# Second w1 block issued from ScalarE's queue, and six h groups instead of four on the first 256 rows

## The chip, the cores and the metric

The kernel runs on one core of one Trainium2 chip. The metric is the device time of one execution in microseconds, as the median of several executions. All ratios compare a kernel with executions of the kernel before on the same chip in the same rounds.

## The reference

A dense layer with Silu, forward and backward, in bf16, with x of 2048 × 640, w1 of 640 × 1536 and w2 of 1536 × 640:

```python
h = jnp.einsum("bsd,df->bsf", x, w1)
a = jax.nn.silu(h)
out = jnp.einsum("bsf,fd->bsd", a, w2)
# and the gradients of out for x, w1 and w2, given grad_out
```

## The kernel before

The chip's engines are named: TensorE multiplies matrices, ScalarE and VectorE work element by element, SyncE issues loads. "The engines" without a name are the 16 DMA engines, which move the data; a load "lands" when the last of them has reported its part, and an engine that is far behind the others is called a straggler. A "queue" or "ring" is the list of loads that one issuing engine has handed to them.

The kernel goes through the 2048 rows in four chunks of 512. For each chunk it computes h (12 groups of 128 columns of w1, each with 5 matmuls over D = 5 × 128), then Silu and its derivative, then the output and the gradient of x. The two weight gradients follow. Only the start matters here: the first chunk has to wait for its loads. All of them go through SyncE's queue, in this order:

```python
early += load_x() + [load_w1_rows(0, 1), load_w1_rows(1, 3)]   # x rows 0-255; w1 rows, columns 0-511
load_w1_rows(3, DT)
nc.sync.dma_start_transpose(out=xT_next[:, :, HC:SC], in_=x2[HC:SC, :])   # x rows 256-511, transposed
start_before_entry_wait(nc, {i.ins.name for i in early})
for fc in range(1, NFC):
    load_w1(fc * FC, (fc + 1) * FC)                            # second and third block of 512 columns
nc.scalar.activation(warm_a[:], warm[:, 0:1], ACT.Silu)        # brings the table in early
nc.sync.dma_start(out=w2_nat[:], in_=w2_v[:])
```

TensorE begins with what arrives first: h groups 0 to 3 on the first 256 rows ("half-width" matmuls, 256 columns wide), then the same groups on the other 256 rows, then groups 4 to 11 at full width (512):

```python
def h_first(xT, aT, ghT):
    # ... one tile each for the first FB = 4 groups ...
    for dt_ in range(DT):
        for ft in range(FB):
            h_mm(hps[ft], ft, xT, dt_, dt_ + 1, slice(0, HC))
    for i in range(FT + LAG_G):
        if i < FT:
            if i < FB:
                h_mm(hps[i], i, xT, 0, DT, slice(HC, SC))
            else:
                # ... a new tile ...
                h_mm(hps[i], i, xT, 0, DT)
            silu_a(i, hps[i], aT)
        # ... the derivative of group i - LAG_G ...
```

"Rows 1 and 2" and "rows 3 and 4" below are the second and third of the three loads of w1 rows (row blocks 1-2 and 3-4 of five). "The block" is the second column block of w1, which groups 4 to 7 need.

Of the kernel before, what the change touches and what calls it, by code (L numbers as in the profile page):

```python
# [9 lines left out]
ACT = mybir.ActivationFunctionType  # L10
# [5 lines left out]
def start_before_entry_wait(nc, names):  # L16




    def move(nc):
        blocks = nc.m.functions[0].blocks
        entry, home = blocks[0].instructions, blocks[1].instructions
        for engine in {i.engine for i in home if i.name in names}:
            mine = [i for i in home if i.engine == engine]
            last = max(k for k, i in enumerate(mine) if i.name in names)
            moved = mine[: last + 1]
            gate = next(
                k
                for k, i in enumerate(entry)  # L30
                if i.engine == engine and isinstance(i, mybir.InstEventSemaphore)
            )
            taken = {i.name for i in moved}
            for k in reversed(range(len(home))):
                if home[k].name in taken:
                    del home[k]
            for i in reversed(moved):
                entry.insert(gate, i)

    nc.at_finalize(move)  # L40

# [21 lines left out]
def kernel(  # L63
# [11 lines left out]
    nc = tc.nc  # L75
# [9 lines left out]
    ST, DT, FT = S // P, D // P, F // P  # L85
# [3 lines left out]
    FC = 512  # L89
    NFC = F // FC  # L90
    FB = FC // P
    LAG = 2
    LAG_G = 4
    NWARM = 24
    HC = 2 * P
    dt_in = x.dtype

# [14 lines left out]
    w1_v = w1.rearrange("(dt p) f -> p dt f", p=P)  # L112
# [19 lines left out]
    with ExitStack() as mctx:  # L132
# [7 lines left out]
        warm = cpool.tile([P, P], dt_in, name="warm")  # L140
        early = [nc.vector.memset(warm[:], 1.0)]
        warm_a = cpool.tile([P, 1], FP32, name="warm_a")
        wp = ps_h.tile([P, SC], FP32, name="wp", tag="hp")
        for i in range(NWARM):
            early.append(nc.tensor.matmul(wp[:, 0:P], lhsT=warm[:], rhs=warm[:], start=True, stop=True))
# [4 lines left out]
        w1_nat = w1pool.tile([P, DT, F], dt_in, name="w1_nat", tag="w1a")  # L150
# [14 lines left out]
        xT_next = xpool.tile([P, DT, SC], dt_in, name="xT")  # L165
        x_two = cpool.tile([P, 2, D], dt_in, name="x_two")

        def load_w1(lo, hi):
            nc.sync.dma_start(out=w1_nat[:, :, lo:hi], in_=w1_v[:, :, lo:hi])

        def load_x():
            return [nc.sync.dma_start(out=x_two[:], in_=x2[0:HC, :].rearrange("(p q) d -> p q d", q=2))]

        def load_w1_rows(lo, hi):
            return nc.sync.dma_start(out=w1_nat[:, lo:hi, 0:FC], in_=w1_v[:, lo:hi, 0:FC])  # L175

        early += load_x() + [load_w1_rows(0, 1), load_w1_rows(1, 3)]
        load_w1_rows(3, DT)
        nc.sync.dma_start_transpose(out=xT_next[:, :, HC:SC], in_=x2[HC:SC, :])  # L179
        start_before_entry_wait(nc, {i.ins.name for i in early})  # L180
        for fc in range(1, NFC):
            load_w1(fc * FC, (fc + 1) * FC)
        nc.scalar.activation(warm_a[:], warm[:, 0:1], ACT.Silu)
        nc.sync.dma_start(out=w2_nat[:], in_=w2_v[:])
        goT_next = load_goT(0)
        for fc in range(NFC):
# [3 lines left out]
        for dt_ in range(DT):  # L190
# [3 lines left out]
            copy_tp = nc.scalar.copy if dt_ % 2 else nc.vector.tensor_copy  # L194
            copy_tp(out=xT_next[:, dt_, 0:HC], in_=tp[:].rearrange("p q s -> p s q"))

        def h_mm(hp, ft, xT, lo, hi, cols=slice(0, SC)):
            for dt_ in range(lo, hi):
                nc.tensor.matmul(  # L199
                    hp[:, cols],  # L200
                    lhsT=w1_nat[:, dt_, ft * P:(ft + 1) * P],
                    rhs=xT[:, dt_, cols],
                    start=(dt_ == 0),
                    stop=(dt_ == DT - 1),
                )

        def silu_a(ft, hp, aT):
            nc.scalar.activation(aT[:, ft, :], hp[:], ACT.Silu)  # L208

        def silu_grad(ft, hp, aT, ghT):  # L210
            t = tpool.tile([P, SC], FP32, name="t")
            nc.scalar.activation(t[:], hp[:], ACT.Tanh, scale=0.5)  # L212
            v = tpool.tile([P, SC], dt_in, name="v")
            nc.vector.tensor_scalar(out=v[:], in0=t[:], scalar1=-0.5, scalar2=0.5, op0=ALU.mult, op1=ALU.add)  # L214
            nc.vector.scalar_tensor_tensor(  # L215
                out=ghT[:, ft, :], in0=aT[:, ft, :], scalar=1.0, in1=v[:], op0=ALU.subtract, op1=ALU.mult
            )
# [6 lines left out]

        def h_first(xT, aT, ghT):
            hps = []
            for ft in range(FB):
                hps.append(ps_h.tile([P, SC], FP32, name="hp"))
            for dt_ in range(DT):
                for ft in range(FB):  # L230
                    h_mm(hps[ft], ft, xT, dt_, dt_ + 1, slice(0, HC))
            for i in range(FT + LAG_G):
                if i < FT:
                    if i < FB:
                        h_mm(hps[i], i, xT, 0, DT, slice(HC, SC))
                    else:
                        hps.append(ps_h.tile([P, SC], FP32, name="hp"))
                        h_mm(hps[i], i, xT, 0, DT)
                    silu_a(i, hps[i], aT)
                if i >= LAG_G:  # L240
                    silu_grad(i - LAG_G, hps[i - LAG_G], aT, ghT)
# [35 lines left out]
        for c in range(NCH):  # L277
            xT, goT = xT_next, goT_next
# [13 lines left out]
            if c == 0:  # L292
                h_first(xT, aT, ghT)
                nc.sync.dma_start(
                    out=aT_scr[:, c * SC:(c + 1) * SC].rearrange("(ft p) s -> p ft s", p=P), in_=aT[:]
                )
                sd_phase(c, w2_nat, aT, oT_scr)
                for ft in range(FT):
                    g_group(ft, goT, ghT)
                nc.sync.dma_start(  # L300
                    out=ghT_scr[:, c * SC:(c + 1) * SC].rearrange("(ft p) s -> p ft s", p=P), in_=ghT[:]
                )
                sd_phase(c, w1T, ghT, gxT_scr)
                continue

            for i in range(FT + LAG):
# [7 lines left out]
                out=aT_scr[:, c * SC:(c + 1) * SC].rearrange("(ft p) s -> p ft s", p=P), in_=aT[:]  # L314
            )
            nc.sync.dma_start(
                out=ghT_scr[:, c * SC:(c + 1) * SC].rearrange("(ft p) s -> p ft s", p=P), in_=ghT[:]
# [7 lines left out]
    with ExitStack() as fctx:  # L325
# [17 lines left out]
        k = 0  # L343
# [26 lines left out]
        k = 0  # L370
        for fc in range(NFC):
            gh_blk = gh_blks[fc]
            for dt_ in range(DT):
                if dt_ == DT // 2:
                    store_gw2(fc)
                if fc == NFC - 1 and dt_ == DT - 1:
                    for k, (lo, hi) in enumerate(((0, FC - P), (FC - P, FC))):
# [12 lines left out]
                        else:  # L390
                            nc.vector.tensor_copy(out=g1[:, lo:hi], in_=gp[:, lo:hi])  # L391
                        last_store = nc.sync.dma_start(
                            out=gw1_v[:, dt_, fc * FC + lo:fc * FC + hi], in_=g1[:, lo:hi]
# [49 lines left out]
```

## Time and profile before

| | before |
|---|---|
| time, median (lowest to highest) | 321.23 us (320.87 to 321.48, 4 executions) |
| profiled span | 319.2 us, clock 1.000 |
| TensorE busy | 314.0 us, 98% of the span |
| TensorE's only long wait after its first load | 9.19 to 9.88 us, for the block |
| block: issued, landed | 3.90, 9.83 us |
| second half of xT: issued, landed | 1.99, 6.9 us |
| first matmul of the first output group | 18.52 us |

The last line is a useful mark: everything that the change touches lies before it, and the profile shows no wait of TensorE after it, so a shift of this mark is a shift of the end (in the result the mark moves by 3.70 us and the span from 319.2 to 322.9). The three loads of w1 rows have a view of their own; its last line gives the times from issue to landing:

```profile
L175 SPq DMA_DIRECT2D w_nat<-in_w_dram x3: 378/411/434, 0.5 to 1.6; - x3
...
DMA to landing us min/median/max: 3.0/3.6/4.1
```

They are issued at 0.54, 1.00 and 1.57 us and land at 3.5, 4.6 and 5.6.

### The profile page before, as it was taken

To read this page: it belongs to the slowest core of one execution; us is meant where nothing else is said; L and a number is where in the kernel's file an instruction comes from. 1 tells how busy PE (TensorE), PEld (TensorE's weight loads), DVE (VectorE), ACT (ScalarE), POOL (GpSimd) and SP (SyncE) were. 2 spreads that over 40 slices of the span, in tenths; PEclk is the share of its full clock that TensorE was granted. 3 is DMA by queue.
4 is the path that set the end of the run, shared out by engine and by line. 5 is a ranking of instruction groups with operands and counts; after the bars stand their busy time and mean duration, and the time that the engine had idled before them with its cause. 6 is when DMAs were issued, how large, how long until landed. Compare 5 with 4: busy or idle time off the path is not lost.

```text
span 319.2 us, 3567 instructions
## 1 busy us (share of the span) xinstructions
PE 314.0 (98%) x1481; PEld 147.2 (46%) x1510; DVE 101.1 (32%) x179; ACT 77.1 (24%) x140; POOL 0.7 (0%) x6
## 2 busy tenths in 40 slices
PE   9999999999999999999999999999999999999996
PEld 8444444444444444444444444444444444444443
DVE  1771641477410187710147741000000100001001
ACT  3951000545201354411064420110100001000100
POOL 0000000000000000000000000000000000000000
PEclk9999999999999999999999999999999999999999
DMA  8999999999899868292534079819999999995011
GB/s 230 351 185 212 253 264 254 366 257 305 230 289 313 215 194 166 90 304 83 166 114 132 2 262 267 213 34 292 267 240 271 256 224 329 283 236 170 33 38 46
DMA packets 148480, 67.35 MB, mean 211 GB/s; under 512 B 113904, under 2 KB 148336, under 8 KB 148464
## 3 DMA queue, kind: packets, MB, share of 16 engines
q1 hardware_dynamic: 148464, 67.12, 81.4%
q8 instruction: 12, 0.20, 0.2%
q14 instruction: 4, 0.03, 0.0%
HBM read 9.50 MB, written 28.97 MB: 121 GB/s over the span
## 4 chain that ended last, share of the span: by engine, by line
PE 96%; DMA 2%; SPq 1%; issue 1%; DVE 0%; DVEq 0%
PE hp L262 32%; PE hp L246 16%; PE hp L350 16%; PE hp L399 15%; PE hp L199 15%; DMA w_nat<-in_w_dram 2%; PE hp L380 1%; SPq L179 1%; SPq L175 0%; DVE g L391 0%; DVEq L391 0%
## 5 line engine op out<-in xcount | busy, mean ns | idle before, releaser
L199 PE MATMUL hp<-xT,w_nat 128*128 128x512 bf16 (+1 forms) x252 | 57.2, 365 | 0.9 <-DMA w_nat<-in_w_dram 0.5
L246 PE MATMUL hp<-goT,w2T 128*128 128x512 bf16 x238 | 56.8, 379 | 0.1
L262 PE MATMUL hp<-ghT,w1T 128*128 128x512 bf16 x235 | 52.2, 379 | 0.3
L262 PE MATMUL hp<-aT,w_nat 128*128 128x512 bf16 x236 | 52.2, 379 | 0.2
L350 PE MATMUL hp<-a_blk,go_nat 128*128 128x512 bf16 x235 | 51.7, 379 | 0.3
L399 PE MATMUL hp<-gh_blk,x_nat 128*128 128x512 bf16 x219 | 48.1, 379 | 0.2
L270 ACT ACTIVATE oT<-hp 128x512 bf16<-128x512 f32 x24 | 14.3, 597 | 110.0 <-PE hp L262 110.0
L199 PEld LDWEIGHTS <-w_nat 128*128 128x128 bf16 x260 | 25.6, 99 | 27.3 <-DMA w_nat<-in_w_dram 0.8
L208 ACT ACTIVATE aT<-hp 128x512 bf16<-128x512 f32 x48 | 28.7, 604 | 33.4 <-PE hp L199 33.4
L262 PEld LDWEIGHTS <-w1T 128*128 128x128 bf16 x240 | 23.5, 98 | 28.3
L262 PEld LDWEIGHTS <-w_nat 128*128 128x128 bf16 x240 | 23.5, 98 | 28.3
L350 PEld LDWEIGHTS <-go_nat 128*128 128x128 bf16 x240 | 23.4, 98 | 28.4
L246 PEld LDWEIGHTS <-w2T 128*128 128x128 bf16 x240 | 23.4, 98 | 28.4
L272 DVE CAST oT<-hp 128x512 bf16<-128x512 f32 x16 | 11.1, 691 | 77.3 <-PE hp L262 65.7
L253 DVE SCALAR_TENSOR_TENSOR ghT<-ghT,hp 128x512 bf16<-128x512 bf16 x48 | 32.5, 682 | 7.3 <-PE hp L246 7.3
L399 PEld LDWEIGHTS <-x_nat 128*128 128x128 bf16 x224 | 21.9, 98 | 26.5
L215 DVE SCALAR_TENSOR_TENSOR ghT<-aT,v 128x512 bf16<-128x512 bf16 x48 | 32.5, 685 | 0.3
L214 DVE TENSOR_SCALAR v<-t 128x512 bf16<-128x512 f32 x48 | 20.2, 426 | 31.5 <-ACT t L212 31.5
L212 ACT ACTIVATE t<-hp 128x512 f32<-128x512 f32 x48 | 28.6, 601 | 0.0
L410 DVE CAST g<-hp 128x512 bf16<-128x512 f32 x7 | 4.8, 691 | 47.0 <-PE hp L399 24.0
L360 DVE CAST g2T<-hp 128x512 bf16<-128x512 f32 x7 | 4.8, 692 | 46.1 <-PE hp L350 39.9
L358 ACT ACTIVATE g2T<-hp 128x512 bf16<-128x512 f32 x8 | 4.8, 597 | 47.0 <-PE hp L350 47.0
(20 smaller groups left out, 23.2 us busy)
## 6 DMA issues: line engine op xcount, KB each, us to landing
aT_scr<-aT SPq DMA_DIRECT2D x4, 1536.0 KB, 6.6
ghT_scr<-ghT SPq DMA_DIRECT2D x4, 1536.0 KB, 10.0
out_dram<-o_sb SPq DMA_DIRECT2D x8, 640.0 KB, 3.4
oT_scr<-oT SPq DMA_DIRECT2D x4, 640.0 KB, 4.4
go_nat<-in_grad_out_dram SPq DMA_DIRECT2D x4, 640.0 KB, 6.5
x_nat<-in_x_dram SPq DMA_DIRECT2D x4, 640.0 KB, 6.2
gxT_scr<-oT SPq DMA_DIRECT2D x4, 640.0 KB, 4.8
w_nat<-in_w_dram SPq DMA_DIRECT2D x1, 1920.0 KB, 12.0
```

The costliest lines, as they stand in the source:

```text
L199: nc.tensor.matmul(hp[:, cols], lhsT=w1_nat[:, dt_, ft * P:(ft + 1) * P], rhs=xT[:, dt_, cols], start=(dt_ == 0), stop=(dt_ == DT - 1),)
L208: nc.scalar.activation(aT[:, ft, :], hp[:], ACT.Silu)
L212: nc.scalar.activation(t[:], hp[:], ACT.Tanh, scale=0.5)
L214: nc.vector.tensor_scalar(out=v[:], in0=t[:], scalar1=-0.5, scalar2=0.5, op0=ALU.mult, op1=ALU.add)
L215: nc.vector.scalar_tensor_tensor(out=ghT[:, ft, :], in0=aT[:, ft, :], scalar=1.0, in1=v[:], op0=ALU.subtract, op1=ALU.mult)
L246: nc.tensor.matmul(gp[:], lhsT=w2T[:, dt_, ft * P:(ft + 1) * P], rhs=goT[:, dt_, :], start=(dt_ == 0), stop=(dt_ == DT - 1),)
L253: nc.vector.scalar_tensor_tensor(out=ghT[:, ft, :], in0=ghT[:, ft, :], scalar=1.0, in1=gp[:], op0=ALU.add, op1=ALU.mult)
L262: nc.tensor.matmul(op_[:], lhsT=w_all[:, ft, dt_ * P:(dt_ + 1) * P], rhs=rhs_all[:, ft, :], start=(ft == 0), stop=(ft == FT - 1),)
L270: nc.scalar.activation(oT[:, dt_, :], op_[:], ACT.Copy)
L272: nc.vector.tensor_copy(out=oT[:, dt_, :], in_=op_[:])
L350: nc.tensor.matmul(gp[:], lhsT=go_nat[:, st, dt_ * P:(dt_ + 1) * P], rhs=a_blk[:, st, :], start=(st == 0), stop=(st == ST - 1),)
L399: nc.tensor.matmul(gp[:], lhsT=x_nat[:, st, dt_ * P:(dt_ + 1) * P], rhs=gh_blk[:, st, :], start=(st == 0), stop=(st == ST - 1),)
```

## The change

The intent: the block should not stand behind the slow issue of the transposing load (1.86 us in the profile before), so it goes on ScalarE's queue, right behind the small activation that loads the table. And TensorE should have more to do before it needs the second half of xT, so six groups run on the first 256 rows.

```diff
+def issue_behind(nc, late, first):
+    # ... moves instruction `late` to the place just behind `first` on the same engine ...
...
+    NHG = 6
...
+        table = nc.scalar.activation(warm_a[:], warm[:, 0:1], ACT.Silu)
+        issue_behind(nc, load_w1(nc.scalar, 1).ins.name, table.ins.name)
         start_before_entry_wait(nc, {i.ins.name for i in early})
-        for fc in range(1, NFC):
-            load_w1(fc * FC, (fc + 1) * FC)
-        nc.scalar.activation(warm_a[:], warm[:, 0:1], ACT.Silu)
+        for fc in range(2, NFC):
+            load_w1(nc.sync, fc)
...
-            for ft in range(FB):
+            for ft in range(NHG):
                 hps.append(ps_h.tile([P, SC], FP32, name="hp"))
             for dt_ in range(DT):
                 for ft in range(FB):
                     h_mm(hps[ft], ft, xT, dt_, dt_ + 1, slice(0, HC))
+            for ft in range(FB, NHG):
+                h_mm(hps[ft], ft, xT, 0, DT, slice(0, HC))
             for i in range(FT + LAG_G):
                 if i < FT:
-                    if i < FB:
+                    if i < NHG:
                         h_mm(hps[i], i, xT, 0, DT, slice(HC, SC))
```

More of the change, by code (lines that the diff above doesn't have):

```diff
@@ L38, in move @@
                 entry.insert(gate, i)
+    nc.at_finalize(move)
+def issue_behind(nc, late, first):
+    def move(nc):
+        home = nc.m.functions[0].blocks[1].instructions
+        at = next(k for k, i in enumerate(home) if i.name == late)
+        inst = home[at]
+        assert not inst.sync_info.on_wait
+        del home[at]
+        behind = next(k for k, i in enumerate(home) if i.name == first)
+        assert home[behind].engine == inst.engine
+        home.insert(behind + 1, inst)
     nc.at_finalize(move)
@@ L166, with load_w1 @@
         x_two = cpool.tile([P, 2, D], dt_in, name="x_two")
-        def load_w1(lo, hi):
-            nc.sync.dma_start(out=w1_nat[:, :, lo:hi], in_=w1_v[:, :, lo:hi])
+        def load_w1(eng, fc):
+            cols = slice(fc * FC, (fc + 1) * FC)
+            return eng.dma_start(out=w1_nat[:, :, cols], in_=w1_v[:, :, cols])
         def load_x():
```

## The prediction

> **What bounds the kernel now.** I read the busy shares first, then the chain of work that ended last, then the timeline and the stretches of the first 22 us. The page of the kernel before:
>
> ```profile
> PE 314.0 (98%) x1481; PEld 147.2 (46%) x1510; DVE 101.1 (32%) x179; ACT 77.1 (24%) x140; POOL 0.7 (0%) x6
> ...
> PE 96%; DMA 2%; SPq 1%; issue 1%; DVE 0%; DVEq 0%
> ```
>
> TensorE is busy for 98% of the span and makes up 96% of the chain. Going through its matmul records one by one, I find no idle time between 10 us and the end except one missing record about every 50 matmuls. So the change, which touches only the first 18 us, can win only what TensorE idles there. The chain of the first 22 us shows how much that is:
>
> ```profile
> 1.99 1.86 SPq L179
> 3.85 0.05 issue
> 3.90 5.94 DMA w_nat<-in_w_dram
> ...
> 9.88 0.39 PE hp L199
> ```
>
> The columns are start, duration and piece. The issue of the transposing load of the second half of xT (L179) holds SyncE's queue until 3.85 us; only then is the second column block of w1 issued, and it lands 5.94 us later, at 9.84. The first matmul of the fifth h group starts at 9.88. In the timeline of TensorE:
>
> ```profile
> 6.03 3.33 PE L199 MATMUL hp<-xT,w_nat 128*128 128x256 bf16 x29
> 9.88 0.82 PE L199 MATMUL hp<-xT,w_nat 128*128 128x512 bf16 x2 [0.53 <-DMA w_nat<-in_w_dram]
> ```
>
> The half-width (256-column) matmuls start 0.109 us apart once the clock is full. The last of the 40 starts at 9.08, so the next could have started at 9.19. The true loss is 9.88 − 9.19 = **0.69 us**[...]. That is 0.2% of 321.05, and it is all there is to win. The DMA engines decide whether it is won:
>
> ```profile
> 3.00:4.00 1.00, 0.95 (x10) 0.71 (x8) 0.28 (x1) 0.07 (x1) 0.00 (x0) 1.00 0.81 230
> 4.00:5.00 1.00, 1.00 (x10) 0.81 (x8) 1.00 (x3) 0.68 (x2) 0.00 (x0) 1.00 0.99 302
> 5.00:6.00 1.00, 1.00 (x9) 0.84 (x8) 0.00 (x0) 0.00 (x0) 0.00 (x0) 1.00 1.27 253
> 6.00:7.00 1.00, 1.00 (x11) 0.89 (x10) 0.00 (x0) 0.00 (x0) 0.00 (x0) 1.00 1.07 256
> ```
>
> The last two columns are the share of DMA time and GB/s: from 4 us on the engines are full, and even from 3 to 4 they stand at 0.81.
>
> [...]
>
> **The change, part by part.** *Earlier issue.* ScalarE's queue: the table load runs from 0.74 to 2.02, the small activation from 2.03 to 2.24, so the load of the w1 block issues at about 2.25 rather than 3.90. That is 1.65 us earlier. SyncE also loses one issue (0.58 us), so the third w1 block and w2 are issued that much earlier, but they wait for the engines anyway. ScalarE's next work, two copies of xT at 3.94, should stay clear of an issue of about 0.6 us.
>
> *New order of the matmuls.* Two more groups (4 and 5) run on the first 256 rows between the 20 half-width matmuls of groups 0 to 3 and the ones for the last 256 rows. In all, 10 full-width matmuls become 20 half-width ones: 20 × 0.109 − 10 × 0.2158 = +0.02 us, with the weight loads (98 ns) still under the matmul (109 ns). The needs move. The first 20 matmuls end at 7.01 in the kernel before; there it needs the second half of xT, which landed at 1.99 + 4.9 = 6.9, and at 9.19 it needs the w1 block. After the change it needs the w1 block at **7.01**, and the second half of xT 10 matmuls later, at **8.10**. So the load is issued 1.65 us earlier but needed 2.18 us earlier; in exchange the transposing load may be 1.1 us later.
>
> *What the engines can deliver.* The order of the two landings changes, not the bytes. In the record of landings, 12 of the 16 engines finish the w1 block by 8.71 and four stragglers between 9.40 and 9.84 (two of its packets, at 6.3 us, took 0.84 and 0.98 us, beside a usual 0.05). So all bytes up to the w1 block are moved by about 8.7, if no straggler shows up. The changed kernel needs the same bytes by 8.10. The slack that the second ring could use is the fifth of the engines that idled from 3 to 4 us, about 0.2 us, so both should be there at about 8.5: a wait of roughly **0.4 us** at the xT half or before, in place of 0.69. The sum of this: −0.69 + 0.02 + 0.4 ≈ **−0.3 us**.
>
> *ScalarE behind it.* The first Silu moves from 7.76 to about 8.85, because h group 0 completes ten matmuls later. ScalarE then runs 24 activations every 0.48 to 0.5 us. The twelfth Silu has 21 before it in the new order (22 before), so it is done at about 19.6. The first output group needs it at its twelfth matmul: 17.9 + 11 × 0.216 = 20.2. So this margin shrinks from about 1.6 us to about 0.6, and it holds. w2 landed at 17.4 and will be needed at about 17.7 in place of 18.3: also narrow, also enough.
>
> **The rivals.** *A. Clean win.* The w1 block lands by 7.0 and xT by 8.1, and TensorE never waits: 321.05 − 0.69 + 0.02 = 320.4. For it speaks that somebody chose six groups, so has probably seen how the two landings lie[...]. Against it: the engines are full.
> *B. The wait moves into the first rows.* [...] About 440 packets of the first block's rows are then left; beside as many of the other ring, at some 280 packets per us, they end at about 6.3 rather than 4.9. Rows 3 and 4 are needed at 6.14 and landed at 5.63. With the 0.6 us from last packet to landing this would be 6.9, a wait of 0.75 us; later needs shift with it and are then met. Net +0.1: 321.1.
> *C. The issue is held up,* [...]. The block then lands at 8 to 9.8 but is needed at 7.0: a wait of 1 to 2.8 us in place of 0.69. Net +0.3 to +2.1: 321.4 to 323. Against it: [...]x_two's issue took only 0.39.
> *D. ScalarE or w2 becomes late* by the 0.7 us that TensorE is ahead: then the gain is given back in the first output group, and the time is 320.8 to 321.0. The margins worked out above speak against it.
>
> **Range and chances.** I give A about 0.35, the middle case of −0.3 about 0.3, B and D together 0.25, C 0.1. The middle of these is about 320.7. The low end is A plus the scatter of the timed runs (0.2 us below their median at the least): 320.2. The high end takes in B and a mild C: 321.7. A step of 2% is 6.4 us, nine times what TensorE idles in the whole stretch, so faster by that is ruled out by the sum, and slower by it would need a stall that nothing here suggests, such as a reordered load that comes late in a later chunk. The other loads have margins of microseconds: the weights w1T landed at 38.2 and are needed at 44.2, the first block of a at 203.8 and needed at 212.9.
>
> **What would show it.** Right: in the timeline, the block's issue on ScalarE at about 2.25, its landing before 8.7, no wait of over 0.5 us at the first matmul of group 4, and the sum of TensorE's waits from 4 to 14 us at about 0.4. The first matmul of the first output group then starts at about 18.2 (18.52 before). For A it would start at 17.9; for B a wait shows between the matmuls at 5.2 and 6.6 us; for C, the ScalarE issue is long or the landing at over 8.7; for D, a wait in the first output group for ScalarE or w2. Wrong: a first output group that starts later than 18.5, or a time that moves without it moving.

The marks here and in the expectations of e7, e9 and e13 show where passages are cut that stated behaviour of the hardware which nothing measured in this case had shown: a paragraph on how loads of two issuing engines share the DMA engines and on the spacing of matmuls, a clause on the 0.53 in brackets (it counts from the recorded end of the last matmul, 9.35), the first step of rival B, and one reason in A and two in C. (The spacing is in the profile before: 0.109 us for 256 columns from 5.5 us on, 0.213 until 5.2 us; 0.216 for 512 columns.) The sum came to −0.69 + 0.02 + 0.4 ≈ −0.3 us. Its 0.4 is the author's estimate; that a second queue would use the engines' idle fifth had not been shown (from 3 to 4 us their share was 0.81 before and 0.97 in the changed kernel). Rival B counts from about 3.2 us, 0.9 us after the issue, and gives the block and the rows equal shares of the engines, also an assumption; it came to 6.3 us for the last packet of the rows and 6.9 for their landing.

## The result

The changed kernel takes **324.59 us** (324.20 to 324.83, 4 executions), before 321.23: 1.0% slower, ratio 1.0104 with a 95% interval of 1.0087 to 1.0122. A ratio is the mean time of one kernel's fast runs over that of the other's of the same rounds, so it is not quite the ratio of the medians quoted. Executions over 1.5% slower than the fastest of the same kernel are left out of the means. The page of the changed kernel, lines that answer to those of before, with the clock that was granted to TensorE in 40 slices and the group of the h matmuls:

```profile
PE 315.8 (98%) x1492; PEld 149.0 (46%) x1520; DVE 101.2 (31%) x179; ACT 76.8 (24%) x140; POOL 0.7 (0%) x6
...
PEclk9799999999999999999999999999999999999999
...
PE 96%; DMA 2%; issue 1%; DVE 0%; DVEq 0%
...
L219 PE MATMUL hp<-xT,w_nat 128*128 128x512 bf16 (+1 forms) x262 | 58.9, 365 | 2.9 <-DMA w_nat<-in_w_dram 2.5
```

The shares look as they did. The news is in two places: the h matmuls now wait 2.9 us in total, mainly for w1, and in the second slice (8 to 16 us) the clock is at 0.7. The timeline of the first 10 us (start, duration, engine, line, what):

```profile
0.73 1.28 ACT L199 ACT_TABLE_LOAD   x1 [0.73 <-DVEq L449]
0.79 0.44 ACTq L188 DMA_DIRECT2D w_nat<-in_w_dram  x1
...
1.99 3.69 SPq L198 DMA_TRANSPOSE xT<-in_x_dram  x1
2.02 0.20 ACT L199 ACTIVATE warm_a<-warm 128x1 f32<-128x1 bf16 x1
...
7.32 1.05 PE L219 MATMUL hp<-xT,w_nat 128*128 128x256 bf16 x8 [1.98 <-DMA w_nat<-in_w_dram]
...
8.91 11.31 PE L219 MATMUL hp<-xT,w_nat 128*128 128x256 bf16 x67 [0.54 <-DMA w_nat<-in_w_dram]
```

The load stands behind the table load and the activation in program order, but it was issued at **0.79 us**, while the table load ran until 2.02 and the activation started only then. So in this run the issue waited for the end of neither. The prediction had looked at the queue as if the load had to wait for the engine.

The waits are not for the block but for the first w1 rows. Their view in the changed kernel:

```profile
L194 SPq DMA_DIRECT2D w_nat<-in_w_dram x3: 378/413/434, 0.5 to 1.6; - x3
...
DMA to landing us min/median/max: 3.0/6.3/7.3
```

The issues are where they were (1.00 and 1.57 us). Rows 1 and 2 land at 7.28 (4.61 before), rows 3 and 4 at 8.87 (5.63 before). The chain of the first 14 us has one piece where the kernel before had the xT issue and the block:

```profile
1.57 7.30 DMA w_nat<-in_w_dram
8.87 0.05 issue
8.91 5.14 PE hp L219 x31
```

In the stretches (the last three columns are granted clock, DMA share and GB/s; a packet's whole time counts in the share of the stretch where it starts, which gives the 2.89) of the same kernel, and then one stretch of the kernel before:

```profile
6.00:7.00 1.00, 0.00 (x0) 0.00 (x0) 0.00 (x0) 0.00 (x0) 0.00 (x0) 1.00 2.89 239
7.00:8.00 1.00, 0.68 (x7) 0.61 (x8) 0.00 (x0) 0.00 (x0) 0.00 (x0) 1.00 0.64 77
8.00:9.00 1.00, 0.46 (x5) 0.18 (x3) 0.00 (x0) 0.00 (x0) 0.00 (x0) 0.89 0.57 108
9.00:10.00 1.00, 1.00 (x6) 0.69 (x7) 0.00 (x0) 0.00 (x0) 0.00 (x0) 0.50 1.19 279
...
12.00:13.00 1.00, 1.00 (x10) 0.86 (x9) 0.00 (x0) 0.00 (x0) 0.00 (x0) 0.91 1.07 362
```

```profile
7.00:8.00 1.00, 1.00 (x12) 0.89 (x10) 0.00 (x0) 0.25 (x1) 0.00 (x0) 1.00 0.98 316
```

Two more things appear. From 7 to 9 us, where TensorE's two waits end, the engines move only 77 to 108 GB/s, where the kernel before moved 316 and 349. And from 8.78 to 12.19 us TensorE's clock is at 0.50: 3.41 us. In the 3.4 us before (5.36 to 8.78) TensorE stood still for about 2.5. What sets the start and the length of the half clock, the profile does not show.

The first output group starts at 22.22 us, 3.70 later than before. In the timelines of TensorE, before and after:

```profile
18.52 2.75 PE L262 MATMUL hp<-aT,w_nat 128*128 128x512 bf16 x12
22.22 2.97 PE L284 MATMUL hp<-aT,w_nat 128*128 128x512 bf16 x13
```

Worked out from the matmul records, in us:

| term | us |
|---|---|
| the wait at group 4, now gone | −0.69 |
| 20 half-width for 10 full-width matmuls | +0.02 |
| wait for rows 1 and 2: 7.323 − 4.931 − 0.213 | +2.18 |
| wait for rows 3 and 4: 8.912 − 8.097 − 0.109 | +0.71 |
| half clock while busy, 8.91 to 12.19: 3.28 / 2 | +1.64 |
| sum | +3.86 |
| measured, 22.22 − 18.52 | +3.70 |

Of the difference, 0.04 is an earlier first matmul and 0.08 is one matmul less among those of the start, which come 0.213 us apart; 0.04 stays.

### The profile page after: what moved, and what is told of

The parts are those of the page before. It is cut to its first block, busy times and chain, and to the rows that moved or that the text cites. A ratio compares the mean times of both kernels' runs of the same rounds, so it can differ in the third digit from the quotient of the medians.

```text
span 322.9 us, 3588 instructions
## 1 busy us (share of the span) xinstructions
PE 315.8 (98%) x1492; PEld 149.0 (46%) x1520; DVE 101.2 (31%) x179; ACT 76.8 (24%) x140; POOL 0.7 (0%) x6
## 4 chain that ended last, share of the span: by engine, by line
PE 96%; DMA 2%; issue 1%; DVE 0%; DVEq 0%
PE hp L284 32%; PE hp L219 16%; PE hp L268 16%; PE hp L372 16%; PE hp L421 15%; DMA w_nat<-in_w_dram 2%; PE hp L402 1%; DVE g L413 0%; DVEq L413 0%
## 5 line engine op out<-in xcount | busy, mean ns | idle before, releaser
L219 PE MATMUL hp<-xT,w_nat 128*128 128x512 bf16 (+1 forms) x262 | 58.9, 365 | 2.9 <-DMA w_nat<-in_w_dram 2.5
L219 PEld LDWEIGHTS <-w_nat 128*128 128x128 bf16 x270 | 27.3, 102 | 29.3 <-DMA w_nat<-in_w_dram 3.3
L228 ACT ACTIVATE aT<-hp 128x512 bf16<-128x512 f32 x48 | 29.4, 622 | 38.9 <-PE hp L219 38.9
L284 PEld LDWEIGHTS <-w_nat 128*128 128x128 bf16 x240 | 23.4, 98 | 28.4
L232 ACT ACTIVATE t<-hp 128x512 f32<-128x512 f32 x48 | 29.3, 631 | 0.0
```

The lines of the kernel that those rows point to most:

```text
L219: nc.tensor.matmul(hp[:, cols], lhsT=w1_nat[:, dt_, ft * P:(ft + 1) * P], rhs=xT[:, dt_, cols], start=(dt_ == 0), stop=(dt_ == DT - 1),)
L228: nc.scalar.activation(aT[:, ft, :], hp[:], ACT.Silu)
L232: nc.scalar.activation(t[:], hp[:], ACT.Tanh, scale=0.5)
L284: nc.tensor.matmul(op_[:], lhsT=w_all[:, ft, dt_ * P:(dt_ + 1) * P], rhs=rhs_all[:, ft, :], start=(ft == 0), stop=(ft == FT - 1),)
```

## The experiments

My theory after this: the block, issued at 0.79 us, takes DMA time from the rows that TensorE needs first; the long wait then halves the clock. Rivals: the order of the matmuls is to blame; a second queue is harmful in itself; the clock costs nothing. Here are all runs (us; median, lowest to highest, fast runs; "one look" is a single execution):

| run | time | ratio to before (95%) |
|---|---|---|
| e1 order alone | 323.01 (322.95 to 325.56), one slow run of 336.37 left out | 1.0078 (1.0034 to 1.0122) |
| e9 order alone, again | 324.03 (323.01 to 325.28) | 1.0088 (1.0059 to 1.0117) |
| e2 queue alone | 324.16 (322.68 to 325.51) | 1.0087 (1.0048 to 1.0126) |
| e3 issue gated | 326.77 (325.48 to 328.43) | 1.0187 (1.0151 to 1.0222) |
| e4 waits filled | 323.19 (323.16 to 323.31) | 1.0059 (1.0044 to 1.0074) |
| e5 gated, transposing load later | 326.83, one look | |
| e6 one ring, order of need | 322.45 (321.98 to 323.00) | 1.0041 (1.0022 to 1.0059) |
| e8 other ring, old time | 323.82 (321.92 to 324.78) | 1.0076 (1.0044 to 1.0108) |
| e10, e12 transposing load far away | 331.86 and 332.73, one look each | |
| e13 half the block on ScalarE's queue | 321.50 (321.27 to 323.17) | 1.0032 (0.9995 to 1.0069) |
| e7 split block, one ring | 320.81 (320.63 to 321.44) | 0.9994 (0.9980 to 1.0007) |
| e11 split block and split w2, one ring | 320.47 (320.34 to 320.52) | 0.9976 (0.9963 to 0.9990) |

All of them gave correct results.

### The two parts alone (e1, e9, e2)

e1 and e9 are one kernel: the changed kernel with the block back on SyncE's queue.

```diff
-        issue_behind(nc, load_w1(nc.scalar, 1).ins.name, table.ins.name)
-        for fc in range(2, NFC):
+        for fc in range(1, NFC):
             load_w1(nc.sync, fc)
```

> The six-group order alone; the second w1 block stays on SyncE's queue. My theory (the queue, not the order, made the loss): the first w1 rows land as in the kernel before (by 4.6 and 5.6 us), no wait there. The order brings the need of the block forward to 7.0 us while it lands at about 9.8, so a wait of about 2.8 us stands before group 4; after it 40 half-width matmuls are left where the kernel before had only full-width ones, so about +2.2 us: 323.4. If the wait halves TensorE's clock for 3.4 us as it did in the changed kernel, +3.3. Rival (the order is harmless, as the 0.02 us of the prediction says): 321.2.

> The six-group order alone once more, since the profile of its first run fell in a slow state and its times scattered. Theory: the block lands at 9.8 to 10.2 us as in the kernel before, but is needed at 7.0; the first output group starts about 2.2 us late. Runs whose granted clock is 1.0 take 323.0, runs with 0.995 about 1.7 to 2.6 us more[...]. Rival: all runs within 0.5 us of each other, with or without the lower clock.

e2 is the changed kernel with four groups first:

```diff
-    NHG = 6
+    NHG = 4
```

> The move to ScalarE's queue alone, four groups first as before. My theory: the block is issued at about 0.8 us, shares the engines with the first w1 rows, which land at about 7.3 and 8.9 in place of 4.6 and 5.6; TensorE waits about 2.2 and 0.7 us and then runs 3.4 us at half clock. The whole loss is there: 324.5, within 0.3 of the changed kernel. Rival (the new order shares the loss): under 323.5.

Each part alone costs nearly what both cost together. For the order alone, the timeline of TensorE (e9, profiled run of 325.28 us):

```profile
5.14 2.03 PE L218 MATMUL hp<-xT,w_nat 128*128 128x256 bf16 x16 [0.46 <-DMA w_nat<-in_w_dram]
10.24 9.45 PE L218 MATMUL hp<-xT,w_nat 128*128 128x256 bf16 x54 [3.08 <-DMA w_nat<-in_w_dram]
```

The first rows are nearly on time (6.07 for rows 3 and 4, 5.63 before), but the block lands at 10.20 and TensorE, which now needs it at 7.0, stands for 3.1 us. So the theory "the queue, not the order" was wrong: the new order by itself turns a wait of 0.69 us into one of 3. The clock goes with the scatter here: of the seven fast executions, the four with a granted clock of 1.0 took 322.95 to 323.19, the three with 0.995 took 324.87 to 325.56. What decides between the two was not shown (only one fast run of the order alone has a profile, with a clock of 0.69 from 10 to 12 us and 0.50 from 12 to 14); the groups are about 2 us apart.

In the queue alone rows 3 and 4 land as in the changed kernel (8.84 us), rows 1 and 2 even later (8.10), and TensorE waits 2.88 us, in one piece. The median lies 0.43 below the changed kernel, where the expectation allowed 0.3, and two of the four runs (322.68 and 323.48) meet the rival's number; of these four, the clock does not sort them (325.51 had 1.0), so what makes that scatter stays open.

### The clock (e4)

The changed kernel with unneeded matmuls on data that is there already, in the two waits for w1 rows:

```diff
             for dt_ in range(DT):
+                for _ in range({1: 9, 3: 3}.get(dt_, 0)):
+                    nc.tensor.matmul(hps[FB][:], lhsT=ident[:], rhs=x_two[:, 0, 0:SC], start=True, stop=True)
                 for ft in range(FB):
```

> The changed kernel with 9 and 3 unneeded 512-column matmuls of data that is there, in the two waits for w1 rows. The loads are not touched. My theory (of the 3.4 us, about 1.6 come from the half clock from 8.8 to 12.2 us that follows the long wait): the granted clock stays at 1.0, the landings stay at 7.3 and 8.9, and the first output group starts about 1.6 us earlier, at 20.6: 322.9. Rival (the clock has another cause, or costs nothing because TensorE waits anyway): 324.5 or slower.

The stretches of e4, to be set beside those of the changed kernel, and its first output group:

```profile
8.00:9.00 1.00, 0.95 (x8) 0.62 (x7) 0.00 (x0) 0.00 (x0) 0.00 (x0) 1.00 0.52 112
9.00:10.00 1.00, 1.00 (x11) 0.88 (x10) 0.00 (x0) 0.00 (x0) 0.00 (x0) 1.00 1.26 294
...
20.84 1.46 PE L286 MATMUL hp<-aT,w_nat 128*128 128x512 bf16 x6
```

The clock stays at 1.00, the rows still land at 7.55 and 8.96, and the first output group starts at 20.84, 1.38 us earlier. The median falls from 324.59 to 323.19, and all four runs lie within 0.15 us. So about 1.4 of the 3.4 us lost are the half clock, which nothing in the prediction allowed for. (Counted from the landing of the last rows, which is 0.10 us later here, the gain is 1.48 us, near the 1.64 of the table.) Unneeded work made the kernel faster.

### The time of issue (e3)

The activation writes one column of the block, which the load overwrites. Now the load waits for the activation: it was issued at 2.27 us, and the activation ran from 2.03 to 2.23 (an assertion in `issue_behind`, that the load waits for nothing, is taken out as well):

```diff
-        table = nc.scalar.activation(warm_a[:], warm[:, 0:1], ACT.Silu)
+        table = nc.scalar.activation(w1_nat[:, 0, FC:FC + 1], warm[:, 0:1], ACT.Silu)
```

> As the changed kernel, but the block's load waits for the small activation behind the table load (which now writes one column of the block that the load overwrites), so that it issues at about 2.25 us as the prediction assumed. My theory (the time of issue decides): the issue moves from 0.8 to 2.25, rows 1 and 2 of the first block land before 5.3, rows 3 and 4 at about 6.9; a wait of about 0.75 us, no half clock: 321.1, at most 322. Rival (two rings at once are harmful whatever the time of issue): over 323.5.

The block's issue on ScalarE's queue, the view of the w1 rows (as above, of the same three loads) and the timeline of TensorE in e3:

```profile
2.27 0.42 ACTq L187 DMA_DIRECT2D w_nat<-in_w_dram  x1
```

```profile
L193 SPq DMA_DIRECT2D w_nat<-in_w_dram x3: 379/413/434, 0.5 to 1.6; - x3
...
DMA to landing us min/median/max: 3.0/4.2/4.6
```

```profile
5.21 2.05 PE L218 MATMUL hp<-xT,w_nat 128*128 128x256 bf16 x16 [0.41 <-DMA w_nat<-in_w_dram]
10.48 9.23 PE L218 MATMUL hp<-xT,w_nat 128*128 128x256 bf16 x53 [3.22 <-DMA w_nat<-in_w_dram]
```

This is the kernel that the prediction had in mind: issue at 2.27. The rows are nearly back (5.17 and 6.17 us), which confirms that the early issue had made them late. But the block lands only at 10.43 and xT at 10.64, so TensorE waits over 3 us at group 4 and loses the clock as well (0.66 from 10 to 12 us, 0.50 from 12 to 14): 326.8 us, worse than the changed kernel. The expectation of 321.1 failed, because it held that the same bytes are there by the same time in any order. Two things in the trace's packets speak against that. The block's first packet came at 4.77 us, 2.5 us after its issue; and then, with the transposing load in one ring and the block in the other, the engines moved little:

```profile
6.00:8.00 2.00, 1.26 (x11) 0.70 (x8) 0.00 (x0) 0.00 (x0) 0.00 (x0) 1.00 1.18 205
```

That is 205 GB/s from 6 to 8 us (256 and 316 in the two halves of this stretch in the kernel before). Single packets of the transposing load took up to 0.245 us (0.018 is usual) and of the block up to 0.286 (0.046 is usual); why is not shown.

### Beside what the block travels (e5, e8)

e5 is e3 with SyncE's transposing load moved behind the third w1 block:

```diff
-        nc.sync.dma_start_transpose(out=xT_next[:, :, HC:SC], in_=x2[HC:SC, :])
...
         for fc in range(2, NFC):
             load_w1(nc.sync, fc)
+        nc.sync.dma_start_transpose(out=xT_next[:, :, HC:SC], in_=x2[HC:SC, :])
```

> The gated load of the run before (issue at about 2.3 us on ScalarE's queue), but SyncE issues the transposing load of xT only after the third w1 block, so that beside the block on ScalarE's ring there are only ordinary copies on SyncE's. Theory M (a transposing load in one ring beside a copy in the other is what slows both; in the gated run only 80 to 230 GB/s moved from 5.5 to 7.5 us): the engines move over 300 GB/s from 5 to 8 us, and the block lands by 9.0 us in place of 10.4. Rival R (two rings at once are slow whatever they carry): under 250 GB/s in that stretch and the block at 10 us or later. The time itself is no test here, since the transposing load comes late for TensorE in any case: about 323 to 326.

The block landed at 11.78, not 9.0. The third block, issued 0.3 us earlier on SyncE's queue (1.99), ran ahead of it or beside it; from 6 to 8 us both together moved over 300 GB/s, so in this run the two rings of ordinary copies lost no speed, they divided it. When the transposing load's first packets came (from 7 us on), the rate fell to 39 GB/s at 9.75. Neither theory met it in full.

e8 is the kernel before but for the ring: four groups first, and the block behind ScalarE's first copy of xT, issued at 3.85 us.

```diff
-        issue_behind(nc, load_w1(nc.scalar, 1).ins.name, table.ins.name)
+        late = load_w1(nc.scalar, 1)
...
+            if dt_ == 1:
+                issue_behind(nc, late.ins.name, copied.ins.name)
```

> The kernel before with one thing changed: the second w1 block is issued on ScalarE's queue behind its first copy of xT, at about 3.9 us, the same time as on SyncE's queue before; four groups first. Theory M: the block is beside the transposing load now, both are slowed down; xT lands at over 8.5 us in place of 6.9 (needed at 7.0), the block at over 10; TensorE waits at xT, at least +1.5 us: 322.7 to 326. Rival (the ring does no harm when the first w1 rows are through): block and xT land within 0.5 us of the kernel before, 321.2.

xT landed at 7.34, close to before. That does not refute theory M, though: the block's first packet came only at 6.51 us, when 1246 of the 1280 packets of the transposing load had already started, so the two hardly met. The block landed at 10.78 though it was issued at the old time: the *third* block, which stands behind it on a single ring, came at 3.83 on SyncE's ring and shared the engines with it (from 7.25 to 9.5 us, some 40 packets each in every quarter of a microsecond). In this run a queue of its own gave the block no precedence. It took away the precedence that its place in the one queue gave it (10.78 us against 9.83). (The profiled run is the fastest of the four, 321.92; what the slower three, up to 324.78, waited for was not seen. So theory M, as an account of e3, is not settled.)

### The bytes beside the rows (e13)

The changed kernel, but only the half of the block that groups 4 and 5 need goes on ScalarE's queue:

```diff
-        issue_behind(nc, load_w1(nc.scalar, 1).ins.name, table.ins.name)
+        issue_behind(nc, load_w1(nc.scalar, 1, 0, 2 * P).ins.name, table.ins.name)
...
+        load_w1(nc.sync, 1, 2 * P, FC)
         for fc in range(2, NFC):
             load_w1(nc.sync, fc)
```

> The changed kernel, but only the half of the block that groups 4 and 5 need (256 of 512 columns) goes on ScalarE's queue at 0.8 us; the other half stays on SyncE's queue behind the transposing load. Theory S (the first w1 rows are late by the packets that share the engines with them): with half the bytes beside them, their delay is about half: rows 1 and 2 complete at 5.5 to 6.2 us (7.3 in the changed kernel, 4.6 before), rows 3 and 4 at 6.8 to 7.5 (8.9 and 5.6); TensorE waits about 1.3 us in place of 2.9[...]: 321.8 to 322.4 in every run. Rival (the delay comes from the presence of a second ring or from single slow packets, not from the bytes): rows at 7 and 8.5 us or later as in the changed kernel, over 323.5.

```profile
L194 SPq DMA_DIRECT2D w_nat<-in_w_dram x3: 378/413/434, 0.5 to 1.6; - x3
...
DMA to landing us min/median/max: 3.0/4.8/5.4
```

```profile
5.88 13.06 PE L220 MATMUL hp<-xT,w_nat 128*128 128x256 bf16 x85 [0.50 <-DMA w_nat<-in_w_dram]
18.78 1.46 PE L285 MATMUL hp<-aT,w_nat 128*128 128x512 bf16 x6
```

Rows 1 and 2 land at 5.84, rows 3 and 4 at 7.01: of the delays of 2.67 and 3.24 us, 1.23 and 1.38 are left, a little under half. TensorE waits about 1.0 us, the clock stays at 1.00, and the first output group starts at 18.78. The time is 321.50, below the expected span; of the four runs three lie below it (321.27 to 321.53) and one above (323.17, at clock 1.0 and without a profile). So in these runs the rows are late by the bytes that share the engines with them, not by the second queue as such.

The packets show how unequal that sharing was. In the changed kernel the block is issued 0.2 us before rows 1 and 2, and from 3 to 4 us its ring started 275 packets of 1 KB, SyncE's ring 49; from 4 to 5 us it was 175 and 137. In the kernel before, SyncE's ring alone started 225 from 3 to 4 us.

### The transposing load as a meeting point (e10, e12)

One look at the packets of the changed kernel shows 22 of the 256-byte packets of the transposing load that started between 6.30 and 8.14 us and all ended between 8.60 and 8.68, the longest after 2.35 us (a usual one takes 18 ns). The last rows landed at 8.87. My reading was that engines that reach the transposing load stand still until the last engine has come. The packets that start from 8.14 to 8.59 us fit this: they follow one another like those of a single engine, one of the rows and one of the block in turn until the rows are through (8.33), and from 8.42 on the first of the transposing load; at 8.60 the 22 begin to end. The test moves that load behind w2, in the changed kernel (e10) and in the kernel before (e12):

```diff
-        nc.sync.dma_start_transpose(out=xT_next[:, :, HC:SC], in_=x2[HC:SC, :])
...
         nc.sync.dma_start(out=w2_nat[:], in_=w2_v[:])
+        nc.sync.dma_start_transpose(out=xT_next[:, :, HC:SC], in_=x2[HC:SC, :])
```

> The changed kernel with the transposing load of the second half of xT issued only behind w2 (so xT comes some 10 us late and the time, over 330, is no test). Theory T (the engines that reach the transposing load first stand still there until the last engine has come, and the completions of the w1 rows ahead of it are held until then): without it, the engines move over 280 GB/s in every quarter of a microsecond from 5 to 9 us, where the changed kernel fell to 18 to 110 from 7 to 8.5; rows 3 and 4 land one engine after the other, by 7.5 us, in place of all 16 between 8.71 and 8.87. Rows 1 and 2 still land at 6 to 7.3, since the block still shares the engines with them. Rival (the stragglers are slow on their own account): rows 3 and 4 at 8.5 or later, rate under 150 GB/s from 7.5 to 8.5.

> The same move in the kernel before, as the control: one ring, no transposing load among the first copies (time over 330, no test). Theory T: rows 3 and 4 land one engine after the other between 4.4 and 5.6 us, not 13 of 16 within 0.12 us at 5.5; the block is then finished at about 7.5 us. Rival: rows 3 and 4 still land in one burst at 5.5 us.

The stretches of e10:

```profile
6.00:7.00 1.00, 0.00 (x0) 0.00 (x0) 0.00 (x0) 0.00 (x0) 0.00 (x0) 1.00 1.00 341
7.00:8.00 1.00, 0.00 (x0) 0.00 (x0) 0.00 (x0) 0.00 (x0) 0.00 (x0) 0.95 1.06 376
8.00:9.00 1.00, 0.95 (x5) 0.70 (x6) 0.00 (x0) 0.00 (x0) 0.00 (x0) 0.50 1.08 389
```

The hole is gone: 376 and 389 GB/s where the changed kernel had 77 and 108. So in the changed kernel the hole comes with the transposing load; that engines stand still there is a reading of its packets, not shown more directly. It does not make the rows late, though: without it rows 3 and 4 land one engine after the other, from 6.34 to 9.54 us, and the last is even later. In e12 they land from 4.62 to 6.89 (one by one, as expected; in the kernel before, 13 of 16 engines from 5.51 to 5.63), and the block, expected at 7.5, at 8.64. The stragglers lag on their own account; e10 shows single packets of up to 1.16 us where 0.05 is usual. Slow packets alone don't tell the kernels apart, however: of the 1-KB packets that started before 9 us, 14 took over 0.3 us in e10, 6 in the changed kernel and 10 in the kernel before. Why one engine ends so far behind stays open.

All the runs together show one thing more. Where the block is not issued early on ScalarE's queue, rows 3 and 4 landed at 5.6 to 6.2 us wherever the transposing load came next on SyncE's queue (before, e1, e3, e7, e8, e9, e11), but at 6.9 to 7.2 where an ordinary load did (e5, e6, e12). So a second ring is not needed to make them late; e6 and e12 have none. No experiment was made for this, and its cause is not shown.

What follows is that in the changed kernel the rate fell to 77 GB/s where packets ahead of the transposing load lagged, and the loads issued behind it landed later: the third block at 12.02 us and w2 at 18.94 (11.71 and 17.39 before).

### Orders that might beat both (e6, e7, e11)

e6: six groups, all on SyncE's queue, block before the transposing load.

```diff
         load_w1_rows(3, DT)
+        load_w1(nc.sync, 1)
         nc.sync.dma_start_transpose(out=xT_next[:, :, HC:SC], in_=x2[HC:SC, :])
```

> Six groups first, and all loads on SyncE's ring in the order in which they are needed: w1 rows, second w1 block, transposing load of xT. Theory M: no slowing down; the block lands at about 7.4 us (needed at 7.0), xT at about 8.7 (needed at 8.1 plus the first wait), TensorE waits 0.4 to 0.9 us in all, full clock: 320.8 to 321.4. Rival (the six-group order costs time in itself, as its run alone with +0.8% could be read): over 322.5.

Both landings were missed, and the time with them: rows 3 and 4 landed at 7.18, the block at 9.06, xT at 10.31; TensorE waited 1.06 and 0.83 us at full clock. With six groups x_two, the first block's rows, the second block and the second half of xT, 1.97 MB in all, have to be there by 8.1 us. By then the runs had moved 1.59 to 1.86 MB of anything (e6 1.72), but for e5, e10 and e12, which put the transposing load back (1.90 to 2.02). Not tried were six groups with only the half of the block that they need first, in the one ring.

e7 leaves the kernel before as it is but for two halves of the block:

```diff
-            load_w1(fc * FC, (fc + 1) * FC)
+        load_w1(FC, FC + 2 * P)
+        load_w1(FC + 2 * P, 2 * FC)
+        for fc in range(2, NFC):
+            load_w1(fc * FC, (fc + 1) * FC)
```

> The kernel before with nothing changed but that the second w1 block is loaded as two halves of 256 columns on SyncE's ring, so that groups 4 and 5 have their weights one half earlier. Theory (the 0.69 us before group 4 are the only idle time that can be won, and the first half of the block lands by 8.9 us): no wait at group 4, 320.5, ratio 0.998. Rival (the stragglers that held up the block hold up its first half as well[...]): 321.2, ratio 1.000.

The wait at group 4 was gone, but in the profiled run it came back at the first output group, for w2. TensorE in e7:

```profile
4.30 14.06 PE L201 MATMUL hp<-xT,w_nat 128*128 128x256 bf16 x80
18.98 0.82 PE L264 MATMUL hp<-aT,w_nat 128*128 128x512 bf16 x3 [0.62 <-DMA w_nat<-in_w_dram]
```

w2 landed at 18.94. e11 loads w2 in two halves as well:

```diff
-        nc.sync.dma_start(out=w2_nat[:], in_=w2_v[:])
+        for lo in (0, FT // 2):
+            nc.sync.dma_start(out=w2_nat[:, lo:lo + FT // 2, :], in_=w2_v[:, lo:lo + FT // 2, :])
```

> The split block of its run alone, with w2 loaded in two halves of six row blocks as well. Theory: in the run with the split block alone the 0.69 us at group 4 were won but given back at the first output group, whose w2 landed at 18.95 us where it was needed at 17.9; with the first half of w2 landing at about 14.6 us and the second needed at 19.2, no wait is left: 320.4, ratio 0.9975, interval below 1. Rival (the split costs elsewhere or the wait moves on to the second half): 320.8 to 321.3.

```profile
8.81 9.23 PE L202 MATMUL hp<-xT,w_nat 128*128 128x256 bf16 x43
17.88 5.34 PE L265 MATMUL hp<-aT,w_nat 128*128 128x512 bf16 x23
```

The two halves of w2 landed at 14.57 and 17.99, and the first output group starts at 17.88, 0.64 us before that of the kernel before. The time is 320.47, ratio 0.9976 with an interval below 1: small, but it beats both kernels, and all five runs lie within 0.18 us.

## Why the prediction was wrong

- **What bounds the kernel, and how much is to be won.** Right: TensorE, and 0.69 us at group 4. e11 wins 0.64 of it.
- **"the load of the w1 block issues at about 2.25 rather than 3.90."** This is the first step that failed. It was issued at 0.79, while the table load ran until 2.02. So the block came before rows 1 to 4 of the first block and not behind them: rows at 7.28 and 8.87 in place of 4.61 and 5.63. e3 (issue at 2.27: rows at 5.17 and 6.17) and e13 (half the bytes: a little under half the delay) show it.
- **"The order of the two landings changes, not the bytes", so both are there at about 8.5.** The second step that failed, and it would have failed with the right time of issue: e3 had the block at 10.43 and xT at 10.64. Two terms were wrong there. The block's first packet, which rival B puts 0.9 us after the issue, came 2.5 us after it. And the estimate took the engines' rate as given, while e3 moved 205 GB/s from 6 to 8 us, for a cause that stays open. In the changed kernel the rate failed in another way: it fell to 77 GB/s at the transposing load (376 without that load there, in e10). In e8 the rate was some 350 GB/s from 7.25 us on, but the block shared it with a later load, some 40 packets each per quarter of a microsecond.
- **The needs, 7.01 for the block and 8.10 for xT.** Right, and underrated. The order alone costs 0.8% (e1, e9), because the block is needed 2.2 us earlier and nothing brings it earlier. The prediction wrote +0.02 for the order; that is its cost in matmuls, not in waits.
- **Rival B, the wait in the first rows.** The right place and cause, with a wrong size: its wait of 0.75 us came out as 2.18 + 0.71, since the block was in the engines from 2.8 us on, among rows 1 to 4 and not only behind most of them, and took far more than the equal share that B gave it (275 packets to 49 from 3 to 4 us); and a term was missing: the half clock, 1.64 us in the records and 1.4 by e4. B, C and the middle case all left that out. A wait was counted at its length, while the waits of 2.18 and 0.71 us here cost the half clock besides.
- **Rival C, the issue held up.** Not in the changed kernel (0.44 us for the issue). But the block's first packet came 2.0 us after its issue in the changed kernel and 2.5 us in e3, where x_two's came after 1.0. What held the block's packets longer, the traces don't tell.
- **Rival D, ScalarE or w2 late.** Not in the changed kernel, since TensorE was late itself. But e7 shows it: w2 at 18.94, with the gain given back.
- **The range.** The change was "within 2%" as predicted, but the high end of 321.7 had no room for a loss in which several small steps fail at once.

## What to carry to other kernels

A queue in front of the engines was also an order here: the load that moved to another queue lost its place behind and ahead of others and shared the engines with what was in flight (rows 1 and 2 at 7.28 us in place of 4.61; in e8 the block at 10.78 in place of 9.83), so ask which loads it will share with before asking how early it is issued. Program order behind the activation did not delay the issue (0.79 us, with the activation at 2.02); the dependency of e3 did (2.27). In this kernel, bound by TensorE, waits at the start could cost more than their length: in the profiled runs waits of 2.88, 3.08 and 3.22 us (e2, e9, e3), and of 2.18 and 0.71 in the changed kernel, came with a mean clock of 0.995, waits of 1.06 and 0.83 (e6) and 1.10 (e8) with 1.0, and filling the waits in e4 won 1.4 us. Splitting a load where its first half is needed earlier did what moving it could not (0.64 us in e11).
